# Chunked delta-rule attention with an MLP behind it: one inverse for the first chunk pair, keys apart from queries in three steps, chosen buffer slots, and an order of issue taken from a table

## The chip, the cores and the metric

The kernel runs on one core of one Trainium2 chip. The core has TensorE (PE, with its weight loads PEld), VectorE (DVE), ScalarE (ACT), GpSimd (POOL) and SyncE (SP), which here only issues transfers. Each engine works through its own queue in order and waits on semaphores for the others. The metric is device time in microseconds (us) of one execution of the whole program.

## The reference

`attn` is a recurrent state update for 4 x 8 heads over 768 positions with 48 features; `moe` is a two-layer MLP with softplus on the gated readout.

```python
def _attn_ref(q, k, v, beta, g):              # q k v g: (4, 8, 768, 48), beta: (4, 8, 768)
    k_n = k / (np.linalg.norm(k, axis=-1, keepdims=True) + 1e-06)
    for t in range(S):
        readout = np.einsum('bhd,bhde->bhe', q[:, :, t], state)
        y[:, :, t] = g[:, :, t] * readout
        v_old = np.einsum('bhde,bhd->bhe', state, kt)
        state = state + bt[:, :, :, None] * np.einsum('bhd,bhe->bhde', kt, vt - v_old)

def _moe_ref(x, w_in, w_out):                 # x: (3072, 384), w_in: (384, 2048), w_out: (2048, 384)
    h = x @ w_in
    g = np.maximum(h, 0.0) + np.log1p(np.exp(-np.abs(h)))
    return g @ w_out
```

## The kernel before

The 768 positions are cut into 6 steps (`cc` in the code, counted from 0) of two chunks of 64 positions (`cl`). A chunk is solved at once for all 32 heads. For each step the kernel

- squares and sums the keys (ACT `ksq` L401, DVE `ss` L408), takes 1/norm (ACT Sqrt at L425 in steps 0 and 1, later POOL's pow at L445; DVE L454, L455) and scales the keys to f16 `kn` (L467: DVE, in step 1 POOL); POOL casts the queries to `qn` (L488);
- transposes `kn` and `qn` together on PE (L510) into one PSUM buffer `d`, which ACT copies to `kqt` (L533);
- multiplies keys by keys and keys by queries (the grams, L552 and L556). ACT negates the key part into `kk` (L575); the query part goes through a triangular mask into `mt` (DVE L594; in steps 0 and 1 an ACT copy at L617 and POOL's multiply at L628);
- inverts the small triangular matrices: DVE transposes `kk` into `ln` (L651), two multiplies with beta give `nn` (L675), and 15 pairs of multiply and add (`tmp` L686, `tt` L693) substitute row by row. One such run treats the 16 matrices of a chunk or the 32 of both at the same instruction count. In step 0 the two chunks have runs of their own, the first on DVE and the second on POOL; step 1's run is on DVE and the later ones on POOL;
- brings the result to PE (DVE transposes `tn` L719 and `t` L741, ACT copies), completes the inverse there (X at L775, T at L810 and L820, Z at L862 and L865, with ACT copies `xs`, `td`, `z`);
- runs the chain over the chunks: `w` = v minus keys times state (PE L910, DVE L954; in the first chunk only a copy, L928), `u` in two rounds (PE L968 and L1004, ACT copies L992 and L1035), then new state and readout (PE L1048 and L1058, DVE `s` L1105 and `yg` L1123), and the readout transposed (PE L1141, DVE `xt` L1152);
- runs the MLP: `h` (PE L1176), softplus (ACT `ga` L1197), `o` (PE L1214), a copy (DVE `osb` L1236) and the store. In steps 0 and 5 each chunk is a job of its own, in steps 1 to 4 both chunks are one, so a step's first `h` needs both chunks' `xt`.

q, k, v and g come by SP's queue in the order of the `load` calls, two DMAs of 192 KB for each chunk; the weights come by POOL's queue (L341), each behind a load that is named as its dependency. PE, DVE and the rest get the order of their queues from `Plan`: every piece of work is an item with an engine, an estimated cost, dependencies, buffers and a priority, and `Plan.run` places item after item in the order in which a model of the engines would start them, taking the lowest priority among those that are ready. Priorities are written as 100 times the step plus an offset, with exceptions for steps 0 and 1. Buffers are rings: an item takes the next slot in turn.

## Time and profile before

| | us |
|---|---|
| median of 3 runs | 315.22 |
| lowest, highest run | 311.65, 316.7 |
| the profiled execution's own time | 315.01 |
| its span, first to last instruction | 313.2 |
| mean granted TensorE clock in it | 0.88 of full speed |

The profile is of one execution. Engine busy times overlap, so they don't add up to the span. In timelines a row gives the start in us, the busy time, the engine, the line, the operation with output <- input, shapes (partitions x elements) and how many instructions are merged, and in brackets how long the engine had been idle and what ended that. Matmuls are pipelined, so a merged row's busy time is longer than the distance to the next row. The lines that carry the argument are in the prediction.

### The profile page before, as it was taken

Reading aid. Unit: us, or ns where it says so; the run is one execution under the profiler, and the core shown is the slowest. Engines: PE = TensorE matmul, PEld = TensorE weight load, DVE = VectorE, ACT = ScalarE, POOL = GpSimd, SP = SyncE. Lnnn points to the kernel's source line nnn. Section 1 sums busy time; section 2 is a strip of 40 time slices with the busy share of each in tenths; the row PEclk is TensorE's granted clock in tenths of the full one; section 3 lists DMA queues with packets and bytes.
Section 4 is the critical chain, followed back from the end, with each engine's and each line's share of the span. In section 5 each row is a group of like instructions: output and inputs, shape, how many; then the busy total and the mean of one; then the engine's idle time right before and its main releaser. Section 6 shows DMA issues by size and latency. Waiting matters only on the chain.

```text
span 313.2 us, 13945 instructions
## 1 busy us (share of the span) xinstructions
PE 239.3 (76%) x6384; PEld 159.9 (51%) x6384; DVE 146.1 (47%) x276; ACT 162.0 (52%) x292; POOL 126.4 (40%) x232
## 2 busy tenths in 40 slices
PE   0177302486699989979864989998899989999993
PEld 0056202465568655546554655665455545566761
DVE  2529999892440669253461818363025440133001
ACT  2199703248437655883274476727557156631630
POOL 8919596701072046867860620870005810000000
PEclk9999655569589999998975599999699999999999
DMA  8999999999293188801285490651000220021112
GB/s 118 164 170 159 167 171 178 186 171 160 48 165 70 31 151 165 142 12 46 50 130 86 80 128 12 95 110 47 4 2 4 52 52 4 2 55 34 25 45 53
DMA packets 106860, 27.75 MB, mean 89 GB/s; under 512 B 100784, under 2 KB 106032, under 8 KB 106800
## 3 DMA queue, kind: packets, MB, share of 16 engines
q1 hardware_dynamic: 103680, 23.60, 47.3%
q0 software_dynamic: 3120, 3.24, 6.4%
q8 instruction: 50, 0.82, 1.2%
q14 instruction: 10, 0.08, 0.1%
HBM read 25.26 MB, written 4.72 MB: 96 GB/s over the span
## 4 chain that ended last, share of the span: by engine, by line
PE 56%; DVE 14%; POOL 14%; issue 11%; ACT 4%; DVEq 0%; POOLq 0%; ACTq 0%
PE h L1176 19%; PE o L1214 17%; POOL tt L693 4%; POOL tmp L686 4%; PE d L510 3%; DVE ln L651 2%; DVE tmp L686 2%; PE d L910 2%; PE d L1004 2%; PE d L1058 2%; POOL ss L445 2%; DVE tt L693 2%; PE d L820 2%; PE d L968 2%; DVE nn L675 2%
## 5 line engine op out<-in xcount | busy, mean ns | idle before, releaser
L1197 ACT ACTIVATE ga<-h 128x512 f16<-128x512 f32 x96 | 56.8, 601 | 42.6 <-PE h L1176 39.8
L1176 PE MATMUL h<-xt,w_in 128*128 128x512 f16 (+1 forms) x384 | 75.9, 342 | 2.5 <-DVE xt L1152 1.3
L1214 PE MATMUL o<-w_out,ga 128*128 128x384 f16 x384 | 74.2, 336 | 2.5 <-DVE osb L1236 2.4
L1214 PEld LDWEIGHTS <-ga 128*128 128x128 f16 x384 | 36.9, 100 | 27.7 <-issue 6.5
L1176 PEld LDWEIGHTS <-w_in 128*128 128x128 f16 x384 | 36.5, 101 | 25.8 <-issue 5.9
L445 POOL TENSOR_TENSOR ss<-ss,half_c 128x32 f32<-128x32 f32 x4 | 21.8, 5442 | 35.3 <-DVE ss L408 35.3
L1105 DVE TENSOR_TENSOR s<-d,s 128x384 f16<-128x384 f32 x20 | 10.2, 550 | 50.9 <-PE d L1048 50.9
L1236 DVE COPY osb<-o 128x384 f32<-128x384 f32 x24 | 13.2, 551 | 40.1 <-PE o L1214 40.0
L693 POOL TENSOR_TENSOR tt<-tt,tmp 128x30 f32<-128x30 f32 (+7 forms) x75 | 28.2, 376 | 5.9
L686 POOL TENSOR_TENSOR tmp<-nn,tt 128x30 f32<-128x30 f32 (+7 forms) x75 | 28.0, 373 | 5.6
L533 ACT COPY kqt<-d 128x1024 f16<-128x1024 f16 x24 | 23.8, 1015 | 11.0 <-PE d L510 11.0
L408 DVE TENSOR_REDUCE ss<-ksq 128x16 f32<-128x768 f32 x12 | 11.4, 948 | 29.8 <-ACT ksq L401 29.8
L775 PE MATMUL d<-tn,kk 16*32 16x16 f16 x768 | 8.2, 172 | 20.9 <-ACT tn L729 14.8
L575 ACT ACTIVATE kk<-d 128x256 f16<-128x256 f32 x48 | 16.3, 383 | 15.1 <-PE d L556 13.4
L675 POOL TENSOR_TENSOR nn<-ln,beta_l 128x256 f32<-128x256 f16 x10 | 6.1, 632 | 43.3 <-DVE ln L651 43.3
L510 PE MATMUL d<-ident,kn 128*128 128x128 f16 x96 | 12.1, 264 | 12.8 <-DVE kn L467 10.9
L775 PEld LDWEIGHTS <-kk 16*32 16x32 f16 x768 | 7.4, 92 | 22.4 <-issue 22.2
L510 PE MATMUL d<-ident,qn 128*128 128x128 f16 x96 | 12.2, 262 | 8.0 <-POOL qn L488 4.8
L594 DVE TENSOR_TENSOR mt<-d,mask 128x256 f16<-128x256 f32 x32 | 12.0, 412 | 9.7 <-PE d L556 7.5
L992 ACT CAST u<-d 128x384 f16<-128x384 f32 x24 | 10.4, 485 | 11.8 <-PE d L968 11.8
L552 PE MATMUL d<-kqt 48*64 48x128 f16 x384 | 12.4, 243 | 4.9 <-ACT kqt L533 2.5
L510 PEld LDWEIGHTS <-kn 128*128 128x128 f16 x96 | 8.5, 119 | 13.7 <-DVE kn L467 11.0
(73 smaller groups left out, 371.2 us busy)
## 6 DMA issues: line engine op xcount, KB each, us to landing
kf<-in_k_dram SPq DMA_DIRECT2D x24, 192.0 KB, 5.3
qf<-in_q_dram SPq DMA_DIRECT2D x24, 192.0 KB, 5.3
vf<-in_v_dram SPq DMA_DIRECT2D x24, 192.0 KB, 5.1
gf<-in_g_dram SPq DMA_DIRECT2D x24, 192.0 KB, 5.4
out_dram<-osb SPq DMA_DIRECT2D x48, 96.0 KB, 2.2
w_in<-in_moe_w_in_dram POOLq DMA_DIRECT2D x2, 768.0 KB, 7.6
w_out<-in_moe_w_out_dram POOLq DMA_DIRECT2D x1, 1536.0 KB, 18.7
beta_l<-in_beta_dram POOLq DMA_DIRECT2D x8, 12.0 KB, 4.5
```

What stands on the lines that cost most here:

```text
L445: lambda ss=ss, r=r: nc.gpsimd.tensor_tensor(ss.ap[:, r], ss.ap[:, r], half_c[:, r], ALU.pow),
L510: nc.tensor.transpose(o[:, i, :, j], x.ap[:, p, 2 * i : 2 * i + 2].rearrange("p h d -> p (h d)"), ident,)
L533: lambda tp=tp, kq=kq: nc.scalar.copy(kq.ap.rearrange("p n c -> p (n c)"), f16ps(tp.ap)),
L552: nc.tensor.matmul(o[HALF[r], i], x[:, C:], x)
L575: nc.scalar.activation(kk.ap[:, :, u0 : u0 + 7 : 2].rearrange("p x i t -> p i x t"), g.ap.rearrange("p (i x t) -> p i x t", i=NP, x=4)[:, ...
L686: eng.tensor_tensor(t, nn.ap[:, :, j + 1 :, j : j + 1].broadcast_to([P, 2, n, w]), tt.ap[:, :, j : j + 1, 16 : 16 + w].broadcast_to([P, 2, ...
L693: eng.tensor_tensor(rows, rows, t, ALU.add)
L775: nc.tensor.matmul(uv(xp.ap)[QUAD[qd], u], kk.ap[r, 1, u, :], tn.ap[r, u, :])
L1176: nc.tensor.matmul(hp.ap[:, n * b : n * b + n], w_in[:, j, f * P : (f + 1) * P], xt.ap[:, j, t0 : t0 + n], start=(j == 0), stop=(j == 2),)
L1197: lambda hp=hp, o=gb: nc.scalar.activation(o.ap, hp.ap, AF.Softplus),
L1214: nc.tensor.matmul(op.ap[:, :DM], b.ap[:, c + c0 : c + c0 + 128], w_out[:, f, :], start=(f == 0), stop=(f == NF - 1),)
L1236: lambda op=op, ob=ob: nc.vector.tensor_copy(ob.ap, op.ap[:, :DM]),
```

## The change

Line numbers of the changed kernel are those of its own text (its inverse is at L823, L847, L858 and L865, X at L955, `h` at L1360, `o` at L1398).

1. Step 0 has one inverse for both chunks, on DVE; what follows it (copies, X, T, Z) is still split by chunk (`ends`).
2. In steps 0 to 2 keys and queries are transposed apart, each with copies of half the size, and the grams are two items: keys by keys as soon as the keys are there, queries when they come. The key gram writes its upper half in a matmul of its own, so a step has 192 gram matmuls where it had 128. In step 0 half of the copies of keys go to DVE; the masks of steps 0 and 1 go from POOL to DVE. Step 2's `kn` are scaled on POOL.
3. `kk` is no longer cleared by POOL at the start.
4. The keys of step 1 are loaded ahead of the queries of step 0; the first v and g come chunk by chunk; both halves of w_in wait for the first v and g, w_out for the first v of step 1.
5. One of the two copies of `u` in each round goes from ACT to DVE; the first chunk's `w` goes from DVE to ACT.
6. Rings give out the slot that came free first, by number. Priorities come from `RANK`, a table with a row for each kind of work and a column for each step. `Plan.run` may hold ACT or DVE for an item that is due soon (`WAIT`), counts DVE and POOL as slower beside each other, starts three engines as busy (`BUSY`), and has other limits for PE's groups (`RUN`, `BIG`). None of this is an instruction.

```diff
+    def take(self):
+        self.live += 1
+        x = min(self.freed)
...
+RANK = {
+    "norm": [-722, -1709, -1102, -921, -2682, -1201],
...
+    WAIT = 0.373888
+    BUSY = {"POOL": 8.5, "ACT": 2.3, "DVE": 2.5}
+    RUN = 2
+    BIG = 44
...
+                if e in ("ACT", "DVE"):
+
+                    for r, x in cands:
+                        if x.prio < it.prio - 8 and t0 < r < t0 + self.WAIT * it.cost:
+                            t0, it = r, x
...
-    r_mt = ring("mt", 18, [P, NP, C], F16)
-    r_kk = fixed("kk", 2, [P, 2, U, HC], F16, lambda t: nc.gpsimd.memset(t, 0.0))
+    r_mt = ring("mt", 9, [P, H, C], F16)
+    r_kk = ring("kk", 2, [P, 2, U, HC], F16)
...
     load("k", k, r_k, 0)
+    load("k", k, r_k, 1)
     load("q", q, r_q, 0)
-    load("k", k, r_k, 1)
+    load("v", v, r_v, 0, [0])
+    load("g", g, r_g, 0, [0])
+    weights(w_in[:, :, :FH], w1_hbm[:, :, :FH], ("v", 0, 0), 4.5)
+    weights(w_in[:, :, FH:], w1_hbm[:, :, FH:], ("g", 0, 0), 4.5)
+    load("v", v, r_v, 0, [1])
+    load("g", g, r_g, 0, [1])
     load("q", q, r_q, 1)
...
+    load("k", k, r_k, 2)
+    load("v", v, r_v, 1, [0])
+    load("g", g, r_g, 1, [0])
+    weights(w_out, w2_hbm, ("v", 1, 0), 11.0)
...
-        sc_en, sc_eng = ("POOL", nc.gpsimd) if cc == 1 else ("DVE", nc.vector)
+        sc_en, sc_eng = ("POOL", nc.gpsimd) if cc in (1, 2) else ("DVE", nc.vector)
...
+        other = "DVE" if cc == 0 else "ACT"
+        for cl in cls if cc < 3 else ():
+            kqs = [Buf(r_kqt), Buf(r_kqt)]
+            kqt[cl, 0], kqt[cl, 1] = kqs
+            for j, x, x_it in ((1, kn, kn_it), (0, qn, qn_it)):
+                pj = rk("keys", 6) if j else rk("quer")
+                tp = Buf(p_d)
...
+                def gram_k(kqs=kqs, gp=gp, us=us):
+
+
+                    for p, i, r, m in us:
+                        x = kqs[p].ap[FEAT[m], 2 * i + r, C:]
+                        o = gp[m].ap.rearrange("p (n c) -> p n c", c=2 * HC)
+                        nc.tensor.matmul(
+                            o[HALF[r], NP * p + i],
+                            x,
+                            x[:, None, :HC].broadcast_to([D, 2, HC]),
+                        )
+                    for p, i, r, m in us:
+                        x = kqs[p].ap[FEAT[m], 2 * i + r, C + HC :]
+                        o = gp[m].ap.rearrange("p (n c) -> p n c", c=2 * HC)
+                        nc.tensor.matmul(o[QUAD[2 * r + 1], NP * p + i, HC:], x, x)
+
+                def gram_q(kqs=kqs, gp=gp, us=us):
+                    for p, i, r, m in us:
+                        x = kqs[p].ap[FEAT[m], 2 * i + r]
+                        o = gp[m].ap.rearrange("p (n c) -> p n c", c=C)
+                        nc.tensor.matmul(o[HALF[r], NP * p + i], x[:, C:], x[:, :C])
...
-        groups = [[0], [1]] if cc == 0 else [[0, 1]]
+        groups = [[0, 1]]
+        ends = [[0], [1]] if cc == 0 else groups
...
-            on_dve = cc == 1 or (cc == 0 and gr == [0])
+            on_dve = cc < 2
...
             a4 = [
-                add(
-                    "ACT",
+                evac(
+                    "DVE" if m else "ACT",
                     0.5,
```

What the table does to the queues, at three places. DVE at the first inverse (`ln` the transposed L, `nn` the scaled one, `tt` and `tmp` the substitution, `w` the first chunk's right side). Before:

```order
L651 STREAM_TRANSPOSE ln<-kk_104 128x1024
L454 TENSOR_SCALAR ss<-ss 128x16
L455 RECIPROCAL ss<-ss 128x16
L675 TENSOR_TENSOR nn<-ln,beta_l 128x256 x2
L686 TENSOR_TENSOR tmp<-nn,tt_108 128x30
L693 TENSOR_TENSOR tt_108<-tt_108,tmp 128x2x15
L686 TENSOR_TENSOR tmp<-nn,tt_108 128x56
L693 TENSOR_TENSOR tt_108<-tt_108,tmp 128x2x14x2
L651 STREAM_TRANSPOSE ln<-kk_104 128x1024
L928 CAST w_454<-vf 128x384
L928 CAST w_460<-vf 128x384
L686 TENSOR_TENSOR tmp<-nn,tt_108 128x78
```

and now:

```order
L492 TENSOR_SCALAR ss_160<-ss_160 128x32
L493 RECIPROCAL ss_160<-ss_160 128x32
L549 COPY kqt_241<-d_239 128x8x64
L654 TENSOR_SCALAR kk_168<-d_166 128x8x2x32
L823 STREAM_TRANSPOSE ln_387<-kk_168 128x1024
L847 TENSOR_TENSOR nn_416<-ln_387,beta_l 128x256 x2
L858 TENSOR_TENSOR tmp_425<-nn_416,tt_104 128x30
L865 TENSOR_TENSOR tt_104<-tt_104,tmp_425 128x2x15
L858 TENSOR_TENSOR tmp_425<-nn_416,tt_104 128x56
L865 TENSOR_TENSOR tt_104<-tt_104,tmp_425 128x2x14x2
L858 TENSOR_TENSOR tmp_425<-nn_416,tt_104 128x78
L865 TENSOR_TENSOR tt_104<-tt_104,tmp_425 128x2x13x3
```

The second `ln` and the two `w` have left the run, and it reads one `kk` in which both chunks' keys are written by the rows ahead of it.

POOL in the opening, from its first cast of queries on (`kn` scaled keys, `mt` the masks, `ss` the norms, in the rows of L445 and L483 the pow). Before:

```order
L488 CAST qn_100<-qf 128x16x48
L488 CAST qn_101<-qf 128x16x48
L467 TENSOR_TENSOR kn_94<-kf,ss 128x16x48
L488 CAST qn_100<-qf 128x16x48
L628 TENSOR_TENSOR mt<-mt,mask 128x256 x2
L341 DMA w_in<-in_moe_w_in_dram 128x3x1024
L467 TENSOR_TENSOR kn_95<-kf,ss 128x16x48
L488 CAST qn_101<-qf 128x16x48
L628 TENSOR_TENSOR mt<-mt,mask 128x256 x3
L675 TENSOR_TENSOR nn<-ln,beta_l 128x256 x2
```

and now:

```order
L527 CAST qn_100<-qf_120 128x16x48
L505 TENSOR_TENSOR kn_94<-kf_114,ss_160 128x16x48
L527 CAST qn_101<-qf_123 128x16x48
L505 TENSOR_TENSOR kn_95<-kf_117,ss_160 128x16x48
L387 DMA w_in<-in_moe_w_in_dram 128x3x1024 x2
L837 MEMSET tt_104 128x32x16
L838 COPY tt_104<-beta_l 128x2x16
L527 CAST qn_100<-qf_335 128x16x48
L527 CAST qn_101<-qf_120 128x16x48
L387 DMA w_out<-in_moe_w_out_dram 128x16x384
L483 TENSOR_TENSOR ss_1109<-ss_1109,half_c 128x32
```

The masks are gone, both halves of w_in stand together, w_out stands behind the next clearing of `tt_104`, which the first inverse still uses, and the pow of step 2 behind w_out.

POOL at a later pow. Before, where the inverse of step 3 ends:

```order
L686 TENSOR_TENSOR tmp<-nn,tt_108 128x30
L693 TENSOR_TENSOR tt_108<-tt_108,tmp 128x2x15
L445 TENSOR_TENSOR ss<-ss,half_c 128x32
L665 MEMSET tt_108 128x32x16
L666 COPY tt_108<-beta_l 128x2x16
L445 TENSOR_TENSOR ss<-ss,half_c 128x32
L488 CAST qn_100<-qf 128x16x48
```

and now, near the end of the inverse of step 2:

```order
L865 TENSOR_TENSOR tt_105<-tt_105,tmp_425 128x2x3x13
L483 TENSOR_TENSOR ss_128<-ss_128,half_c 128x32
L858 TENSOR_TENSOR tmp_425<-nn_416,tt_105 128x56
L865 TENSOR_TENSOR tt_105<-tt_105,tmp_425 128x2x2x14
L858 TENSOR_TENSOR tmp_425<-nn_416,tt_105 128x30
L865 TENSOR_TENSOR tt_105<-tt_105,tmp_425 128x2x15
L527 CAST qn_101<-qf_335 128x16x48
L527 CAST qn_100<-qf_120 128x16x48
```

The pow of a later step's norms, which stood behind the whole inverse of step 3, with another right behind it, now stands inside step 2's.

More of the change, by code (lines that the diff above doesn't have):

```diff
@@ L23, in __init__ @@
         self.live = 0
-        self.freed = [0.0] * n
-        self.count = 0
+        self.freed = [(0.0, i) for i in range(n)]
+        self.made = {}
+    def take(self):
+        self.live += 1
+        x = min(self.freed)
+        self.freed.remove(x)
+        if x[1] not in self.made:
+            self.made[x[1]] = self.make(x[1])
+        return x[1], self.made[x[1]]
 class Buf:
@@ L71, in run @@
         issued, arrive = 0, [0.0, 0.0]
+        now = {}
+        for e, t in self.BUSY.items():
+            free[e] = t
         mode, run = "full", 9
@@ L128, in run @@
                 if b.ap is None:
-                    r = b.ring
-                    r.live += 1
-                    r.freed.remove(min(r.freed))
-                    b.ap = r.make(r.count)
-                    r.count += 1
-            it.fn()
+                    b.slot, b.ap = b.ring.take()
+            it.fn()
+            cost = it.cost
+            if e == "POOL" or it.sb:
+                x = now.get("DVE" if e == "POOL" else "POOL")
+                if x is not None and x.sb:
+                    cost += 0.5 * max(0.0, min(x.end - t0, cost))
+            now[e] = it
             if it.dma:
@@ L310, with load @@
     tiles = {}
-    def load(name, x, r, cc):
-        for cl in range(2):
+    def load(name, x, r, cc, cls=(0, 1)):
+        for cl in cls:
             b = Buf(r)
@@ L789 @@
             )
-        for gr in groups:
+        for gr in ends:
             us = slice(16 * gr[0], 16 * gr[-1] + 16)
@@ L1096 @@
             )
+            if first:
+                e3[1].order.append(c1)
             if not final:
```

400 lines of the change are left out of this document (253 added, 147 removed).

## The prediction

> **What bounds the kernel now.** I read the page's head and slices first, then busy time by stretch, then the timeline of the two places where TensorE is idle.
>
> ```profile
> span 313.2 us, 13945 instructions
> PE 239.3 (76%) x6384; PEld 159.9 (51%) x6384; DVE 146.1 (47%) x276; ACT 162.0 (52%) x292; POOL 126.4 (40%) x232
> ...
> PEclk9999655569589999998975599999699999999999
> DMA  8999999999293188801285490651000220021112
> ```
>
> TensorE is busy 76% of the span, but the granted clock is 0.5 to 0.6 in slices 5 to 9 and 0.5 in slices 22 and 23. The busy time by stretch (columns: length, then busy us of PE, PEld, DVE, ACT, POOL, then granted clock, DMA share, GB/s):
>
> ```profile
> 0.00:65.30 65.30, 22.28 (x684) 18.02 (x685) 47.13 (x92) 28.43 (x61) 45.48 (x84) 0.76 1.21 165
> 65.30:90.50 25.20, 19.17 (x721) 14.67 (x721) 10.62 (x23) 14.04 (x23) 7.04 (x6) 0.75 0.76 128
> 90.50:153.90 63.40, 59.50 (x1529) 38.53 (x1527) 31.28 (x57) 40.24 (x72) 34.69 (x68) 0.97 0.47 88
> 153.90:178.40 24.50, 15.88 (x729) 13.34 (x730) 14.46 (x26) 11.77 (x17) 12.68 (x9) 0.62 0.53 88
> 178.40:309.60 131.20, 122.43 (x2734) 75.31 (x2732) 42.66 (x81) 67.48 (x120) 26.52 (x67) 0.97 0.23 44
> ```
>
> From 90.5 to 153.9 and from 178.4 on TensorE is busy 94% and 93% at a clock of 0.97: there it is the bound, and only work taken from it would help. The losses are the opening (43 of 65.3 us idle), the stretch behind it (6.0 of 25.2) and the hole at 153.9 (8.6 of 24.5, the rest at 0.62).
>
> ```profile
> 6.73 3.57 POOL L272 MEMSET kk<- 128x2048 f16 x2
> 14.38 1.60 POOL L488 CAST qn<-qf 128x768 f16<-128x768 f32 x2
> 15.26 0.61 PE L510 MATMUL d<-ident,qn 128*128 128x128 f16 x4 [4.75 <-POOL qn L488]
> 23.63 1.90 DVE L651 STREAM_TRANSPOSE ln<-kk 128x1024 f16<-128x1024 f16 x1
> 26.51 5.08 DVE L675 TENSOR_TENSOR nn<-ln,beta_l 128x256 f32<-128x256 f16 x2
> 46.73 1.04 DVE L719 STREAM_TRANSPOSE tn<-tt 128x512 f32<-128x512 f32 x1
> 48.49 0.66 PE L775 MATMUL d<-tn,kk 16*32 16x16 f16 x64 [11.98 <-ACT tn L729]
> 54.77 0.21 PE L865 MATMUL d<-td,kk 32*32 32x32 f16 x3 [2.53 <-issue]
> 61.51 0.31 PE L1048 MATMUL d<-u,kn 64*64 64x48 f16 x8 [3.44 <-issue]
> 65.33 3.33 PE L1176 MATMUL h<-xt,w_in 128*128 128x256 f16 x18 [0.65 <-DVE xt L1152]
> ```
>
> The opening is a chain. POOL clears kk and reaches the queries at 14.38, and the joint transposes of keys and queries wait for them (4.75). VectorE transposes the first L at 23.63 and needs until 46.73 for one chunk's inverse; its two scalings (nn) alone take 5.08 while POOL works on the same kind of tensors, and POOL runs the second chunk's inverse beside it. TensorE then waits 11.98 for tn. From tn to the first h are 18.6 us, 2.53 and 3.44 of them waits that no other engine ends ("issue").
>
> ```profile
> 155.65 5.44 POOL L445 TENSOR_TENSOR ss<-ss,half_c 128x32 f32<-128x32 f32 x1
> 163.03 0.61 PE L510 MATMUL d<-ident,kn 128*128 128x128 f16 x4 [0.97 <-DVE kn L467]
> 178.36 1.49 PE L1176 MATMUL h<-xt,w_in 128*128 128x512 f16 x3
> ```
>
> In the hole the o of step 1 has run out and the first h of step 2 comes 24.5 us later: its second chunk's chain stands in TensorE's queue behind the next keys, which wait for POOL's pow at 155.65.
>
> **The change, part by part.** Prices of VectorE alone, of a gram and of the loads:
>
> ```profile
> 50.79 1.14 DVE L675 TENSOR_TENSOR nn<-ln,beta_l 128x256 f32<-128x256 f16 x2
> 58.14 0.33 DVE L686 TENSOR_TENSOR tmp<-nn,tt 128x128 f32<-128x128 f32 x1
> 67.34 0.22 DVE L686 TENSOR_TENSOR tmp<-nn,tt 128x110 f32<-128x110 f32 x1
> 69.77 0.19 DVE L693 TENSOR_TENSOR tt<-tt,tmp 128x30 f32<-128x30 f32 x1
> 6.90 0.95 DVE L408 TENSOR_REDUCE ss<-ksq 128x16 f32<-128x768 f32 x1 [4.42 <-ACT ksq L401]
> 8.89 0.96 DVE L467 TENSOR_TENSOR kn<-kf,ss 128x768 f16<-128x768 f32 x1
> 9.17 0.84 ACT L401 ACTIVATE ksq<-kf 128x768 f32<-128x768 f32 x1 [1.06 <-DMA kf<-in_k_dram]
> 9.83 4.66 SPq L319 DMA_DIRECT2D kf<-in_k_dram  x4
> 30.85 0.30 PE L556 MATMUL d<-kqt 48*32 48x64 f16 x16
> 43.55 10.30 SPq L319 DMA_DIRECT2D kf<-in_k_dram  x4
> ```
>
> *Start of the inverse.* The keys of both pairs are loaded first. The second half of k lands at about 9.15 (ScalarE's wait at 9.17) and four DMAs take 4.66, so each later chunk follows 2.33 behind: 11.5 and 13.8 for the next keys, 16.1 and 18.5 for the first queries. The clearing of kk (3.57) and the queries leave the path. What gates now is ScalarE's and VectorE's order: the Square of the next keys (0.84) stands ahead of the first kqt copy, so that copy and the second chunk's root wait for 12.4. From reduce to the end of kn VectorE took 2.95 (6.90 to 9.85), so the second kn is at 15.3. Behind it come two of the four-transposes of 0.61, a copy behind the next pair's reduce and reciprocal, the gram (64 matmuls, 1.2 at 0.30 for 16, twice that at half clock) and the copy to kk: I take 5.4 for them, so 20.7 for the one transpose of L, which now waits for both chunks (bounds 19.5, and 23.6, the old start). At 1.90 it ends at 22.6.
>
> *One inverse.* nn costs 1.14. Ten late steps took 2.62 from 67.34 to 69.96, 0.26 each; the widest took 0.36 from start to start behind 58.14. Thirty at about 0.29 are 8.8: it ends at 32.6, against 46.73, and POOL stands still meanwhile, since its next clear of tt waits for it. Bounds: if POOL still took turns, the old 20.2 from 26.51, so 42.8; and 30.5 if all thirty went at the pitch of 0.22.
>
> *From tn to the first h.* Before 18.6. Ahead of the first h the order now has 944 matmuls, 684 before: the second chunk's X and T, the queries' grams and the next pair's. They lie largely where TensorE waits for copies; I take 1 us for them. VectorE also takes half the copies of u, and the masks that were POOL's; ScalarE takes the copies of w. That gives 32.6 + 19.6 = 52.2, or 13.1 earlier. Bounds: without the two issue waits 46; with one more of 3.4 and a late load 58. The load: VectorE's reduce for step 2's keys stands between yg and the new state, and those keys are the fifth load behind the first g (18.5 + 4.7 = 23.2). At 2.33 each they land at 35, at the slowest pace shown (10.30 for four DMAs, beside the weights) at 49, where about 45 is needed.
>
> *The weights.*
>
> ```profile
> w_in<-in_moe_w_in_dram POOLq DMA_DIRECT2D x2, 768.0 KB, 7.6
> w_out<-in_moe_w_out_dram POOLq DMA_DIRECT2D x1, 1536.0 KB, 18.7
> 45.54 1.18 POOL L341 DMA_DIRECT2D w_out<-in_moe_w_out_dram  x1
> 69.83 0.81 PE L1214 MATMUL o<-w_out,ga 128*128 128x384 f16 x4
> ```
>
> w_out was there at 45.54 + 18.7 = 64.2, ahead of its first use at 69.83. It now waits for step 1's first v, the seventh load behind 23.2: 39.5, and with w_in's two 768 KB at the pace of the loads (8 x 1.17) 48.8. So it lands near 67.5. Ahead of the first o stand 398 matmuls behind the first h; at the rate of the third stretch (1529 in 63.4) 16.5, so 68.7. It costs nothing, and that cover is thin: each us beyond it is a us.
>
> *Behind the first h.* The stretch to 90.5 lost 6.0 idle and ran at 0.75. Now it holds no o and one chunk's chain; I take 3 less (bounds 6 less, 3 more).
>
> *The hole.*
>
> ```profile
> 117.74 0.44 PE L910 MATMUL d<-s,kqt 48*64 48x48 f16 x32
> 121.11 1.20 POOL L675 TENSOR_TENSOR nn<-ln,beta_l 128x256 f32<-128x256 f16 x2 [2.05 <-DVE ln L651]
> 137.71 1.25 DVE t L741 x2
> ```
>
> Steps 2 to 4 get keys, pow and gram earlier, and the longest run of matmuls without h or o in the order falls from 728 (24.5 us) to 502, now between steps 0 and 1. By count that is 16.9, so 7.6 less; the 226 moved go between h and o at 0.44 for 32, 3.1 in all. So 4.5 saved (bounds 0, if the new hole is as long, and 14.6, if it closes to its work at full clock: 15.88 at 0.62 is 9.8, of which 502/728 are 6.8; 24.5 - 6.8 - 3.1).
>
> *Added grams.* 192 more matmuls at 0.30 for 16. The first two steps' lie in the opening; the third's 64 cost 1.2, I take 1 (bounds 0 and 3.6). Buffer slots and the planner's new rules issue nothing. The third step's two kn go from VectorE to POOL, idle there.
>
> Sum against the profiled execution: 313.2 - 13.1 - 3.0 - 4.5 + 1.0 = 293.6. Its own time was 315.01, 1.8 more, and stands 0.2 under the median of 315.22. So 295.4, told as 295.
>
> On the issue waits the Trainium skill speaks against me ("Runtime: NRT & Kernel Launch", Instruction fetch mechanics): TensorE's instructions come in blocks and the crossing is "mostly hidden". By it the path from tn would be 6.0 shorter and the time 289; the rows 2.53 and 3.44 show it not hidden while DMA is full, so I keep them.
>
> **The rivals.**
> (a) Nothing waits again: first h at 46 (19.3 gained), 6 behind it, 14.6 in the hole: 313.2 - 19.3 - 6 - 14.6 + 1 + 1.8 = 276, and up to 288 if only part of it comes. For it: in the last stretch no other engine is over 52%. Against: every stretch with small matmuls shows issue waits.
> (b) The hole is only moved: 24.5 us at another place, so 300 (295.4 + 4.5). For it: TensorE runs its queue in order, and the 128 X matmuls of step 2 stand inside the new run.
> (c) The loads bound the opening, since the DMA slices read 9 or more up to slice 10: keys of step 2 at 49, first h at 58: 295.4 + 5.8 = 301, and 304 if w_out is 3 later still. The Trainium skill ("DMA: Bandwidth & Descriptors", Issuing engines are not separate DMA queues) has all queues on the same engines, so that early weights delay the rest; 10.30 against 4.66 agrees.
> (d) Slower: POOL's inverse of step 2 began at 121.11 and its last transposes at 137.71. In the new order the X matmuls of step 2 stand ahead of any h of step 1. 1234 matmuls after the first h the new hole begins, by the same rate at 52.2 + 51 = 103, and X, half-way in it, is due at 111. POOL's inverse now has the next pow (5.44) in its midst, so X is ready 16.6 + 5.4 + 2.4 (transposes, copy) = 24.4 after it starts: a start after 87 delays all that follows, one after 113 makes the kernel slower, and the old 121.11 would give 295 + 34 = 329. Against: its grams stand right behind the first o, with 12 o, the gram, kk and 1.90 of transpose before it, so I expect the start near 77.
> (e) No change: the chain from kn to the first h keeps 60 us or more, 309 to 321; only if VectorE's inverse still takes turns with POOL (10.2 later) and (b) holds.
>
> **How the numbers follow.** Forecast 0.43; (a) 0.18, (b) 0.18, (c) 0.12, (d) 0.03, (e) 0.06. A measurement can tell about 2%, here 308.9 and 321.5. All but (d) and (e) are faster: 0.91; same 0.06; slower 0.03. The range reaches from 281, which leaves out the lower half of (a), to 305: with (d) and (e) 0.18 are outside.
>
> **What would show it.** Right: VectorE's first nn near 1.1, tn near 33, first h between 46 and 58, w_out landed before the first o, POOL's inverse of step 2 before 90, a hole under 20 us between o of step 0 and h of step 1, clock 0.95 or more behind it. Wrong: the inverse over 15 us, X of step 2 waiting for tn, or idle TensorE behind h in a wait for keys.

## The result, and the profile after

| | before | after | predicted |
|---|---|---|---|
| median of 4 runs each, us | 314.62 | 294.69 | 295.0 |
| lowest to highest | 311.65 to 316.7 | 292.62 to 294.87 | 281 to 305 |
| ratio after/before, 95% interval | | 0.938 (0.930 to 0.947) | |
| profiled execution, its span | 315.01, 313.2 | 294.87, 293.2 | |
| first `h` in the profile | 65.33 | 55.15 | 52.2 |
| the hole without `h` or `o` | 24.5 | 17.2 | 16.9 |

A few executions of a kernel run over 1.5% longer than its fastest; the ratio above, and each time and ratio that is given for a run below, is from the mean of the others (before 313.63, the changed kernel 294.22).

The time came out as forecast, but two terms of the sum were off by about 3 us each, in opposite directions, and the experiments show that a part of the gain has another cause than the prediction gave.

The page of the changed kernel, head and slices:

```profile
span 293.2 us, 14316 instructions
PE 236.2 (81%) x6576; PEld 159.3 (54%) x6576; DVE 146.6 (50%) x298; ACT 151.6 (52%) x257; POOL 102.5 (35%) x182
...
PEclk9997555557995995779999999999999999999999
DMA  8999999978989159920297901551100121021212
```

Its busy time by stretch (columns as in the prediction: length, then busy us of PE, PEld, DVE, ACT, POOL, then granted clock, DMA share, GB/s). The stretches are the opening, the one up to the first `o`, the one up to the last `o` of step 0, the hole, and the rest:

```profile
0.00:55.15 55.15, 22.79 (x945) 19.19 (x945) 36.66 (x90) 28.43 (x52) 24.09 (x35) 0.73 1.19 161
55.15:74.40 19.25, 16.72 (x406) 12.68 (x400) 8.89 (x27) 9.65 (x18) 4.01 (x3) 0.61 0.94 155
74.40:106.40 32.00, 28.36 (x838) 18.71 (x835) 16.60 (x29) 15.21 (x25) 19.69 (x38) 0.89 0.65 117
106.40:123.50 17.10, 10.53 (x499) 9.16 (x502) 10.02 (x17) 10.78 (x13) 2.40 (x5) 0.73 0.94 163
123.50:290.00 166.50, 157.79 (x3916) 99.53 (x3908) 74.42 (x137) 87.50 (x150) 52.27 (x104) 0.99 0.29 55
```

From 123.5 on TensorE is busy 157.79 of 166.5 us (95%) at a clock of 0.99; before it was 93% at 0.97. In the 123.5 us ahead of that it is busy 78.4, and the clock is 0.61 to 0.73 in three of the four stretches. The record of the clock begins with its first change, here at 22.26, so the 9s ahead of that are no measurement: eight transposes take 1.04 at 10.81, as long as at 41.80, and 0.61 at 72.11 (rows of the timeline below). So the 0.73 of the first stretch is too high. The timeline of the changed kernel, from VectorE, TensorE and POOL at the places that the prediction named:

```profile
10.81 1.04 PE L566 MATMUL d<-ident,kn 128*128 128x128 f16 x8 [10.81 <-DVE kn L505]
...
20.13 1.92 DVE L823 STREAM_TRANSPOSE ln<-kk 128x1024 f16<-128x1024 f16 x1
22.09 0.76 DVE L847 TENSOR_TENSOR nn<-ln,beta_l 128x256 f32<-128x256 f16 x2
26.99 0.29 DVE L858 TENSOR_TENSOR tmp<-nn,tt 128x128 f32<-128x128 f32 x1
31.63 1.03 DVE L893 STREAM_TRANSPOSE tn<-tt 128x512 f32<-128x512 f32 x1
...
33.38 0.66 PE L955 MATMUL d<-tn,kk 16*32 16x16 f16 x64 [3.72 <-ACT tn L905]
41.80 1.03 PE L566 MATMUL d<-ident,qn 128*128 128x128 f16 x8 [3.63 <-POOL qn L527]
54.13 0.51 PE L1000 MATMUL d<-td,xs 32*16 32x16 f16 x49 [4.07 <-issue]
55.15 2.74 PE L1360 MATMUL h<-xt,w_in 128*128 128x256 f16 x12
60.88 0.39 PE L1148 MATMUL d<-w,td 32*32 32x48 f16 x21 [2.52 <-issue]
65.91 2.74 PE L1360 MATMUL h<-xt,w_in 128*128 128x256 f16 x12
72.11 0.61 PE L566 MATMUL d<-ident,kn 128*128 128x128 f16 x8
74.36 1.95 PE L1398 MATMUL o<-w_out,ga 128*128 128x384 f16 x11
...
43.67 1.18 POOL L387 DMA_DIRECT2D w_out<-in_moe_w_out_dram  x1
80.67 1.20 POOL L847 TENSOR_TENSOR nn<-ln,beta_l 128x256 f32<-128x256 f16 x2 [1.33 <-DVE ln L823]
...
113.57 0.61 PE L955 MATMUL d<-tn,kk 16*32 16x16 f16 x59 [0.34 <-issue]
118.12 0.53 PE L1000 MATMUL d<-td,xs 32*16 32x16 f16 x53 [0.52 <-issue]
123.22 0.52 PE L1090 MATMUL d<-s,kqt 48*64 48x48 f16 x25 [3.68 <-issue]
```

L starts at 20.13 (before 23.63), both nn take 0.76 (5.08), tn is there at 31.63 (46.73). From there to the first `h` are 23.5 us, where 18.6 stood before. The waits that no other engine ends are still there: 4.07 and 2.52 around the first `h`, 3.68 in the hole.

### The profile page after: what moved, and what is told of

It is laid out like the page before. It is cut to its first block, busy times and chain, and to the rows that moved or that the text cites. A ratio compares the mean times of both kernels' runs of the same rounds, so it can differ in the third digit from the quotient of the medians.

```text
span 293.2 us, 14316 instructions
## 1 busy us (share of the span) xinstructions
PE 236.2 (81%) x6576; PEld 159.3 (54%) x6576; DVE 146.6 (50%) x298; ACT 151.6 (52%) x257; POOL 102.5 (35%) x182
## 4 chain that ended last, share of the span: by engine, by line
PE 72%; SPq 11%; issue 8%; DVE 4%; DMA 2%; POOL 1%; ACT 0%; DVEq 0%; POOLq 0%
PE h L1360 24%; PE o L1398 22%; SPq L365 11%; PE d L1090 3%; PE d L1148 2%; PE d L711 2%; PE d L955 2%; PE d L1240 2%; PE d L1000 2%; DMA qf<-in_q_dram 2%; PE d L1045 2%; PE d L1185 2%; PE d L752 2%; PE d L1325 2%; PE d L1230 1%
## 5 line engine op out<-in xcount | busy, mean ns | idle before, releaser
L1360 PE MATMUL h<-xt,w_in 128*128 128x512 f16 (+1 forms) x384 | 77.5, 346 | 0.0
L1398 PE MATMUL o<-w_out,ga 128*128 128x384 f16 x384 | 73.3, 331 | 1.8 <-DVE osb L1420 1.5
L1398 PEld LDWEIGHTS <-ga 128*128 128x128 f16 x384 | 35.7, 99 | 24.3 <-issue 2.9
L1360 PEld LDWEIGHTS <-w_in 128*128 128x128 f16 x384 | 36.9, 103 | 21.7 <-issue 1.1
L549 DVE CAST u<-d 128x384 f16<-128x384 f32 x24 | 13.4, 556 | 37.5 <-PE d L1185 18.9
L483 POOL TENSOR_TENSOR ss<-ss,half_c 128x32 f32<-128x32 f32 x4 | 21.9, 5475 | 28.5 <-DVE ss L446 28.5
L865 POOL TENSOR_TENSOR tt<-tt,tmp 128x30 f32<-128x30 f32 (+7 forms) x60 | 23.5, 392 | 4.7
L858 POOL TENSOR_TENSOR tmp<-nn,tt 128x30 f32<-128x30 f32 (+7 forms) x60 | 21.3, 355 | 4.6
L1134 DVE TENSOR_TENSOR w<-vf,d 128x384 f16<-128x384 f32 x22 | 11.1, 547 | 11.2 <-PE d L1090 10.2
L547 ACT COPY kqt<-d 128x512 f16<-128x512 f16 x22 | 11.9, 590 | 8.3 <-PE d L566 8.3
L439 ACT ACTIVATE ksq<-kf 128x768 f32<-128x768 f32 x12 | 10.2, 846 | 11.6 <-DMA kf<-in_k_dram 9.1
L847 POOL TENSOR_TENSOR nn<-ln,beta_l 128x256 f32<-128x256 f16 x8 | 4.8, 622 | 31.7 <-DVE ln L823 31.7
L1000 PE MATMUL d<-td,xs 32*16 32x16 f16 x768 | 8.6, 167 | 8.9 <-issue 8.8
L1307 DVE TENSOR_TENSOR yg<-d,gf 128x384 f16<-128x384 f32 x24 | 12.2, 547 | 6.2 <-ACT ga L1381 3.5
L734 ACT COPY kqt<-d 128x1024 f16<-128x1024 f16 x12 | 12.1, 1014 | 5.8 <-PE d L711 5.8
L566 PE MATMUL d<-ident,kn 128*128 128x128 f16 x48 | 5.3, 278 | 11.7 <-DVE kn L505 11.7
L527 POOL CAST qn<-qf 128x768 f16<-128x768 f32 x12 | 9.8, 828 | 13.3 <-DMA qf<-in_q_dram 11.2
L955 PE MATMUL d<-tn,kk 16*32 16x16 f16 x768 | 8.1, 171 | 7.0 <-ACT tn L905 3.7
## 6 DMA issues: line engine op xcount, KB each, us to landing
w_out<-in_moe_w_out_dram POOLq DMA_DIRECT2D x1, 1536.0 KB, 15.3
```

Of the source, the lines that this page charges most:

```text
L483: lambda ss=ss, r=r: nc.gpsimd.tensor_tensor(ss.ap[:, r], ss.ap[:, r], half_c[:, r], ALU.pow),
L547: nc.scalar.copy(d, x)
L549: nc.vector.tensor_copy(d, x)
L858: eng.tensor_tensor(t, nn.ap[:, :, j + 1 :, j : j + 1].broadcast_to([P, 2, n, w]), tt.ap[:, :, j : j + 1, 16 : 16 + w].broadcast_to([P, 2, ...
L865: eng.tensor_tensor(rows, rows, t, ALU.add)
L955: nc.tensor.matmul(uv(xp.ap)[QUAD[qd], u], kk.ap[r, 1, u, :], tn.ap[r, u, :])
```

## The experiments

Before's mean beside these runs was 312.67 to 314.11, and 313.63 beside the changed kernel. So times are compared with 294.22 as they stand, and a difference of 1 us is not told apart. The intervals are those of the ratio to before; the changed kernel's is 0.930 to 0.947.

### Which part of the change pays

Two kernels replace the table of order by the rule of the kernel before; the planner then orders everything anew. The second also puts keys and queries back into one transpose.

```diff
-    "norm": [-722, -1709, -1102, -921, -2682, -1201],
-    "pow": [-726, 401, -1276, -1902, -1287, -380],
+    "norm": [-70, -104, 130, 230, 330, 430],
+    "pow": [-120, -154, 80, 180, 280, 380],
...
```

```diff
-        for cl in cls if cc < 3 else ():
+        for cl in cls if cc < 3 and not 0 <= cc < 3 else ():
...
-        for cl in cls if cc > 2 else ():
+        for cl in cls if cc > 2 or 0 <= cc < 3 else ():
```

> The change without its table of order: the ranks are computed by the rule of the kernel before, all other edits stay. Theory T (the gain of the opening comes from the one inverse on VectorE and keys apart from queries, whatever sets the order): first h at 55 to 60, at most 302 us. Rival U (the table makes the gain): first h beyond 60 or a hole of over 24 us again, 308 us or more.

> As the run with the old rule of order, and keys and queries of the first three steps are transposed together again (the split undone). To be held against that run. T: the first transposes wait for the first queries (about 17 in place of 11), the transpose of L starts 2 to 6 later and the time is 2 to 6 us longer. Rival: the second chunk's keys and ScalarE's order gate L anyway, under 1 us.

Measured: 308.10 us, ratio 0.981 (0.970 to 0.992), and 304.50 us, 0.969 (0.959 to 0.980). The first h came at 62.3 and 66.0. So all other edits together are worth about 5 us under the old rule, and the table another 14: rival U holds. The split of keys and queries moves the first h by 3.7 and the time by nothing that can be told apart; the 2 to 6 us longer of T did not come. The table can't be tried without the other edits, which it was made for, so this is no sum of two independent gains.

The granted clock of the run with the old rule bears on half of its 14 us:

```profile
PEclk9997555569999959999959779899999985999999
```

Its first h is 7.2 later than the changed kernel's, and what lies behind it 6.7 longer. There TensorE stands idle as long in both (20.6 us up to 303.0, against 20.1 up to 288.6), but the matmuls take 220.1 us in place of 213.4, and the clock lapses until 262, where the changed kernel's is at half for the last time at 128. The mean clock there is 0.91 against 0.92, too near to account for all of the 6.7.

Two more took back one edit each under the table: two inverses in step 0, and the old order of loads.

```diff
-    r_kk = ring("kk", 2, [P, 2, U, HC], F16)
+    r_kk = fixed("kk", 2, [P, 2, U, HC], F16, lambda t: nc.gpsimd.memset(t, 0.0))
...
-        groups = [[0, 1]]
+        groups = [[0], [1]] if cc == 0 else [[0, 1]]
...
-            on_dve = cc < 2
+            on_dve = cc == 1 or (cc == 0 and gr == [0])
...
```

```diff
     load("k", k, r_k, 0)
+    load("q", q, r_q, 0)
     load("k", k, r_k, 1)
-    load("q", q, r_q, 0)
...
+    weights(w_out, w2_hbm, ("g", 0, 1), 11.0)
...
-    weights(w_out, w2_hbm, ("v", 1, 0), 11.0)
...
```

> The changed kernel with the first step's inverse taken apart again: the first chunk's on VectorE, the second's on POOL, and kk cleared by POOL at the start (L is transposed chunk by chunk). T (the whole pair's inverse on VectorE pays because POOL's half came late and held up VectorE): nn back above 1.5 each, the second chunk's tn behind 50, 3 to 8 us longer than the changed kernel. Rival: the second chunk's chain binds nothing before the first o, within 2 us.

> The changed kernel with the loads in the order of the kernel before (each step whole, w_out behind step 0's g). T: queries of step 0 and keys of step 1 change places, so the first steps of norms come apart, but L hangs on the second chunk's keys of step 0: between 1 us shorter and 4 us longer. Rival (the order of the loads is what lets the inverse start at 20): ln at 23 or later and 3 us or more longer.

Measured: 314.26 us (ratio 1.003, 0.997 to 1.009) and 312.69 us (0.998, 0.994 to 1.003); no theory had this. The edit can't be told from what came with it: with other items the same table gives another order everywhere. The slices of the kernel with two inverses, in its profiled execution (318.29):

```profile
PE   0352479456499985999888799999796999999893
PEclk9996556757579996699959879999659899999999
```

Its first h came at 48.2, 7 us ahead of the changed kernel's, and it is still 20 slower: behind its first 48 h stands a stretch of 30.4 us (56.7 to 87.1) with 692 matmuls and neither h nor o, a second one of 12.4 us follows at 114.7, and the clock reads 5 to 7 in 15 of the 40 slices, where the changed kernel has 11. In the other kernel L even starts earlier, at 19.2, so there the old order of loads did not hold the inverse up; its holes are 22.6 and 12.4 us. An early first h is no gain by itself. Both runs say nothing on the price of their edit, and the later ones therefore keep the changed kernel's order: it is recorded item by item and replayed, with the named edit alone.

### The inverse: what it costs, and why it is short

In one kernel ten reductions of 768 elements stand behind the last step of step 0's inverse on VectorE, in the other 28 multiplies of 128x128 on POOL behind the issue of w_in's second half.

```diff
+    e = [x for x in seq if x.eng == "DVE" and x.cost == 1.4][0]
+    i = seq.index(e.deps[0])
...
+    for n in range(10):
+        x = Item()
+        x.eng, x.bufs = "DVE", []
+        x.fn = lambda: nc.vector.tensor_reduce(pb, pa.broadcast_to([P, 16, 48]), mybir.AxisListType.X, ALU.add)
+        seq.insert(i + 1, x)
```

```diff
+    i = seq.index(wl[1])
...
+    for n in range(28):
+        x = Item()
+        x.eng, x.bufs = "POOL", []
+        x.fn = lambda: nc.gpsimd.tensor_tensor(pb, pb, pa, ALU.mult)
+        seq.insert(i + 1, x)
```

> The changed kernel in its own order on every engine, with ten reductions of 0.95 (nothing uses what they write) behind step 0's inverse on VectorE, so that tn comes about 9.5 later, near the 42.8 at which the prediction's bound for an inverse that takes turns with POOL had it. T (tn sets the start of the rest): 3.6 of it disappear in the wait for step 1's queries at 41.80, so first h 6 later and the time 6 longer (near 301), or up to 9.5. Rival (the issue waits or the loads set the start): first h less than 3 later, time within 2 of the changed kernel.

> The changed kernel in its own order, with 28 multiplications of a 128x128 half-precision tile on POOL (nothing uses them) behind the issue of w_in, beside VectorE's inverse. T (VectorE's nn of 5.08 for two was long because POOL worked on SBUF at the same time): nn back over 1.5 for the two, the inverse over 11 in place of 9.5, time 1 to 5 longer. Rival (nn was long only because of POOL's own inverse and its buffers): nn stays at 0.76, the time the same.

A longer inverse: tn came at 41.65, 10.0 later, the first h at 65.1, 9.9 later, and the time was 301.65 (ratio 0.960, 0.951 to 0.970), 7.4 more. So tn does set the start, and about three quarters of this delay arrive at the end. The wait for the queries at 41.80 was gone, as expected, but the 3.6 did not disappear with it: another wait of TensorE's own (2.88) took its place.

A busy POOL: tn came at 37.84, 6.2 later, the first h at 61.2, 6.1 later, but the first o at 75.9, only 1.6 later, and the time was 295.36 (0.940, 0.930 to 0.951), which can't be told from the changed kernel's. So a delay in the opening does not reach the end by a fixed share. The timelines of VectorE and POOL in that run:

```profile
22.57 0.76 DVE L846 TENSOR_TENSOR nn<-ln,beta_l 128x256 f32<-128x256 f16 x2
23.74 0.48 DVE L864 TENSOR_TENSOR tt<-tt,tmp 128x30 f32<-128x30 f32 x1
30.39 0.47 DVE L857 TENSOR_TENSOR tmp<-nn,tt 128x128 f32<-128x128 f32 x1
36.88 0.47 DVE L864 TENSOR_TENSOR tt<-tt,tmp 128x56 f32<-128x56 f32 x1
37.39 0.19 DVE L857 TENSOR_TENSOR tmp<-nn,tt 128x30 f32<-128x30 f32 x1
37.84 1.03 DVE L892 STREAM_TRANSPOSE tn<-tt 128x512 f32<-128x512 f32 x1
...
23.20 14.08 POOL L1442 TENSOR_TENSOR pb<-pb,pa 128x128 f16<-128x128 f16 x28
```

While POOL's 28 multiplies run (0.427 each, one per 0.50), nearly all of VectorE's take 0.45 to 0.49, whether they have 30 elements or 128, and one comes per 0.51; alone they took 0.19 to 0.29. When POOL is done the next takes 0.19. The two engines take turns, one instruction each. The inverse took 15.3 in place of 9.5. So the mechanism behind the prediction's bound for an inverse that still takes turns is shown, at a smaller price than the bound of 20.2, whose run before also held the second transpose of L and two copies of w: the gain is not the one instruction stream for two chunks alone, but that POOL stands still beside it. Both nn took 0.76 here too, since POOL's multiplies began at 23.20, behind them; so what made nn take 5.08 before was not tried. The Trainium skill ("Trainium Architecture — The Big Picture", What this means for kernel authors) calls the pair's port an exclusive lock, not a split of bandwidth; the equal 0.47 for every size agrees.

### The waits that nobody ends

In each run these waits stand a multiple of 128 matmuls apart. Between the rows 113.57, 118.12 and 123.22 above stand 128 matmuls each; so do 54.13 and 60.88. With a weight load each that is 256 instructions, and the page counts 51 transfers of instructions with 0.84 MB in all, 16 KB each, where 6576 matmuls are 51.4 such blocks. The packed traces date these transfers, and they settle what ends the waits: in all fourteen kernels each of the 224 waits of over 0.3 us at the start of a block ends 1.2 to 1.9 us after a transfer has landed, the first block's after the first transfer, and so on in step. The waits of 4.07 and 2.52 end at 54.13 and 60.88; their transfers landed at 52.59 and 59.47. The planner of both kernels already prices this (3.5 us for each 128 matmuls); the prediction named the fetch and kept the waits, but did not count in blocks. Two kernels move transfers in the recorded order, the queries of step 1 in the first and w_out in the second; a third stands by itself.

```diff
+    four = [tiles[x][1] for x in (("v", 0, 1), ("g", 0, 1), ("q", 1, 0), ("q", 1, 1))]
+    at = [seq.index(x) for x in four]
+    for p, n in zip(at, (2, 3, 0, 1)):
+        seq[p] = four[n]
```

```diff
+    i, j = seq.index(wl[2]), [n for n, x in enumerate(seq) if x.eng == "POOL" and x.cost == 5.6][0]
+    seq.insert(j, seq.pop(i))
```

> The changed kernel in its own order on all engines but SP, where the two loads of step 1's queries stand ahead of v and g of step 0's second chunk. T (those queries, late at POOL, hold TensorE 3.63 at 41.80): that wait goes below 1 and the first h comes 2 to 3.6 earlier, 1 to 3.5 gained in all. Rival (the wait only moves, since v and g come later by as much, or the fetch of TensorE's instructions takes it back): first h within 1 of 55.15 and the time within 1.

> The changed kernel in its own order on all engines but POOL, where the load of w_out stands behind step 2's pow (about 56 in place of 43.7). T (the issue waits of 4.07 and 2.52 are fetches of TensorE's instructions that queue behind w_out's 1.5 MB): they shrink by half, first h 1 to 3 earlier, w_out lands near 71, ahead of the first o at 74.36, 1 to 3 gained. Rival (the loads of q, k, v and g fill the DMA engines anyhow): the waits stay, time within 1, or longer by what w_out comes late.

The first of them failed as an experiment: 299.49 us (0.953, 0.945 to 0.962). The second chunk's queries of step 1 use the buffer of step 0's first chunk, and in this order they are written there before POOL has read it (so this kernel's first chunk works on wrong queries); POOL's first cast waited for that load, 16.46 us until 28.14, and L started at 31.88. Whether the queries of step 1 can profitably come earlier stays open.

The second: 293.30 us, ratio 0.934 (0.926 to 0.942), 0.9 less than the changed kernel, which its interval does not tell apart; the 1 to 3 gained that T expected are not shown. TensorE's timeline there:

```profile
50.02 0.51 PE L999 MATMUL d<-td,xs 32*16 32x16 f16 x49 [0.44 <-issue]
51.03 2.74 PE L1359 MATMUL h<-xt,w_in 128*128 128x256 f16 x12
54.57 0.39 PE L1147 MATMUL d<-w,td 32*32 32x48 f16 x21 [0.32 <-issue]
58.85 0.30 PE L1184 MATMUL d<-u,z 32*32 32x48 f16 x11 [1.24 <-issue]
70.30 2.08 PE L1397 MATMUL o<-w_out,ga 128*128 128x384 f16 x6 [3.16 <-DMA w_out<-in_moe_w_out_dram]
```

The same two matmuls that waited 4.07 and 2.52 now wait 0.44 and 0.32. The 128 between them take 4.55 (50.02 to 54.57) in place of 6.75 (54.13 to 60.88), and the first h comes 4.1 earlier. The rival falls: w_out's 1.5 MB delayed the instructions, although the loads of q, k, v and g fill the DMA engines in both. The transfer itself took 1.05 beside w_out and 1.18 without it; what w_out held up was its start, 4.85 after the block ahead of it began in place of 1.47. A new wait came, of o for w_out until 70.30 (3.16), but that first o is still 4.1 ahead of the changed kernel's, and the first h of step 1 3.8 ahead, at 119.89. Of these 3.8 the profiled execution lost 1.7 behind that h, at a clock of 0.97 where the changed kernel has 0.98.

The kernel by itself issues this twice, 1536 matmuls each, first with no wait on the 24 loads and then behind the last of them:

```python
for i in range(n):
    r = QUAD[i % 4]
    c = 16 * ((i // 4) % 32)
    nc.tensor.matmul(o[r, c : c + 16], x[r.start : r.start + 16, :32], x[r.start : r.start + 16, 32:48])
```

> A kernel by itself that computes nothing of the reference: 1536 matmuls of 16x32 weights by 16 columns while 24 tiles are loaded from q, k, v and g, and 1536 more, with a wait for the last load before them, while nothing is transferred. T (TensorE's instructions come 128 matmuls at a time by DMA and queue behind the loads): in the first part a wait of 2 to 4 before every 128th matmul, in the second part under 1. Rival (the wait hangs on how fast the matmuls are used up, not on the loads): the same wait in both parts.

Its timeline on TensorE, three rows with loads and three without:

```profile
25.36 1.32 PE L48 MATMUL d<-a 16*32 16x16 f16 x128 [3.35 <-issue]
29.91 1.32 PE L48 MATMUL d<-a 16*32 16x16 f16 x128 [3.23 <-issue]
34.74 1.19 PE L48 MATMUL d<-a 16*32 16x16 f16 x128 [3.51 <-issue]
...
71.28 1.19 PE L48 MATMUL d<-b 16*32 16x16 f16 x128 [2.27 <-issue]
75.28 1.19 PE L48 MATMUL d<-b 16*32 16x16 f16 x128 [2.81 <-issue]
79.29 1.19 PE L48 MATMUL d<-b 16*32 16x16 f16 x128 [2.81 <-issue]
```

128 small matmuls take 1.2 to 1.3 us, and the next 128 start 4.55 later on average with loads (51.57 less 6.06, over 10) and 3.73 without (105.11 less 67.83, over 10). So the expectation was wrong and the rival mostly right: the wait is there without any load (2.15 to 2.81), and the loads add 0.8. That the waits look long only where DMA is full comes from what runs there: idle DMA goes with large h and o matmuls, of which 128 last longer than a fetch (13.95 us from 262.58 on). What fits all runs: in a long stretch of small matmuls TensorE gets 128 per 3.7 us with no transfers, per 4.0 to 5.1 beside the loads, and per 6.7 to 7.4 beside w_out (46.69 to 54.13 and 54.13 to 60.88). These are averages of a long stretch: one block is fetched ahead, so the first 223 of the kernel by itself ran without a wait, and in the changed kernel a block of 7.21 (136.01 to 143.22) was followed by one of 2.97.

### The hole and the clock

Three more in the recorded order. In the first w_out comes late, in two halves, and the last 16 o matmuls of step 0 are spread into the hole; in the second five reductions stand ahead of a copy on VectorE; in the third 6, 8 and 8 matmuls stand ahead of three groups of the opening.

```diff
+            nc.gpsimd.dma_start(out=w_out[:, r], in_=w2_hbm[:, r])
...
+    oi = [x for x in pe if x.mm == 4][12:16]
...
+    for x, at in zip(oi, (h[1], h[3], h[6], h[12])):
+        seq.insert(seq.index(at) + 1, x)
```

```diff
+    i = seq.index([x for x in seq if x.eng == "DVE" and x.cost == 0.56][14])
...
+    for n in range(5):
...
+        seq.insert(i, x)
```

```diff
+    for x, n in ((pe[i - 2], 6), (pe[i], 8), (pe[j], 8)):
...
+            for _ in range(n):
+                nc.tensor.matmul(
+                    b.ap.rearrange("p (a c) -> p a c", a=4),
+                    ident,
+                    ident[:, None].broadcast_to([P, 4, P]),
+                )
+            f()
```

> The changed kernel's order with three moves: the load of w_out behind step 2's pow, in two halves (the run with the late load waited 3.16 for the whole of it), and the last 16 o matmuls of step 0 spread into the hole. T: o waits under 1.2 for w_out, the hole's waits of 0.94, 1.08 and 3.68 shrink by 2 to 3 in all under the o between them: 288 to 291. Rival (the hole is paced by VectorE's and ScalarE's copies of step 1, which then come 3.4 after the o as before): 292 to 294, as the run with the late load alone.

> The changed kernel in its own order, with five reductions of 0.95 (nothing uses them) on VectorE ahead of one copy of o near 237, so that TensorE waits about 4 once, in the stretch that ran at a clock of 0.99. T (an idle TensorE loses its clock and pays again when it starts): granted clock near 0.5 for some us behind it, time 6 to 9 longer. Rival: the wait alone, 4 longer, or less if later waits shrink.

> The changed kernel in its own order, with 22 matmuls of 128x128 by 512 that nothing uses, ahead of three groups of the opening that wait 2.65, 3.72 and 3.63 (at about 26, 33 and 42); each writes a PSUM tile that the group then overwrites. T (the opening and the first h run at half clock because TensorE idles): h x12 at 1.48 in place of 2.74 from the start, 3 to 7 gained. Rival (the small matmuls take as long at either clock and waits set the pace): first h within 1 of 55.15, the time within 2; or up to 3 longer where the added ones outlast the waits.

The filled hole: 294.33 us, ratio 0.942 (0.935 to 0.948). No gain over the run with the late load, as its rival said, but not for its reason: the first h of step 1 came at 122.80, and the waits in the hole were again at every 128th matmul (1.33, 0.38, 2.71). The hole is paced by the fetch: two of its waits, 1.33 at 112.69 and 2.71 at 122.34, end 1.4 to 1.7 after a transfer of instructions has landed, and the o matmuls that were put into it count among the 128. w_out's second half was still waited for, 1.61.

The reductions went wrong in place: a cost of 0.56 also marks other work of VectorE, and they ran at 95.2, not near 237. TensorE waited 3.44 at 101.11. Up to there this kernel's order is the changed one's, and yet it was ahead, with the first h at full clock by 65 in place of 70:

```profile
54.29 2.74 PE L1359 MATMUL h<-xt,w_in 128*128 128x256 f16 x12
65.06 1.49 PE L1359 MATMUL h<-xt,w_in 128*128 128x256 f16 x12
71.71 2.11 PE L1397 MATMUL o<-w_out,ga 128*128 128x384 f16 x12
```

So two executions of one order differ by 0.9 at the first h and by 2.65 at the first o. Behind the wait the hole began 1.3 later than the changed kernel's (107.77 against 106.50) and ended 0.5 later (124.19 against 123.67), so it gave back 0.8. The time was 299.39 (0.958, 0.949 to 0.966), 5.2 more, which does not decide between the 4 of the rival and the 6 to 9 of T. In the profiled execution 3.2 us were lost behind the hole, in the clock. The same place in the changed kernel and then in this run:

```profile
194.06 0.18 PE L955 MATMUL d<-tn,kk 16*32 16x16 f16 x3 [1.66 <-issue]
194.18 1.47 PE L1398 MATMUL o<-w_out,ga 128*128 128x384 f16 x8
```

```profile
195.68 0.20 PE L954 MATMUL d<-tn,kk 16*32 16x16 f16 x3 [2.21 <-issue]
195.81 2.74 PE L1397 MATMUL o<-w_out,ga 128*128 128x384 f16 x8
```

After a fetch wait of 1.66 eight o matmuls take 1.47; after one of 2.21 they take 2.74. The granted clock was 1.00 there in the one and 0.50 in the other, from 194.8 to 201.6; at half clock these 6.8 us do the work of 3.4, by this estimate as much as was lost. Which waits cost the clock can't be read off their length alone in these runs.

The added matmuls: 291.05, 293.39, 298.21 and 298.87 us, from which no ratio can be told. In the profiled execution (span 289.3) the first h stayed at 55.36, with a fetch wait of 3.18 before it, but the h that ran at half clock until 70 ran at full clock from 60:

```profile
53.79 0.25 PE L1089 MATMUL d<-s,kqt 48*64 48x48 f16 x3 [3.18 <-issue]
55.36 2.69 PE L1359 MATMUL h<-xt,w_in 128*128 128x256 f16 x12
60.37 1.48 PE L1359 MATMUL h<-xt,w_in 128*128 128x256 f16 x12
70.15 2.11 PE L1397 MATMUL o<-w_out,ga 128*128 128x384 f16 x12
```

The first o came 4.2 ahead of the changed kernel's, but only 1.6 ahead of the one at 71.71 above, which had no matmuls added. What the clock is worth there is therefore not shown: two executions of one order differ by more than half of it, and the four times of this kernel by 8. No version tried beats the changed kernel by more than its runs differ.

## Why the prediction came out right

**Start of the inverse** (20.7, measured 20.13) and **one inverse** (ends 32.6, measured 31.63): right in size and in cause. POOL's turns are shown by the run with the busy POOL. That the keys' loads come first was part of the working; the old order of loads gave 19.2 in another plan, so this step is not shown.

**From tn to the first h** (19.6, measured 23.5): off by 3.9, and the term at fault is the weights. "It costs nothing, and that cover is thin" asked only when w_out lands, not what it holds up. Beside it the two blocks around the first h took 7.44 and 6.75; with w_out later 4.10 and 4.55, and from tn to the first h it was 19.2 (31.88 to 51.03), and 19.7 in the run with the filled hole, as forecast. So the 1 us for 260 more matmuls, two more blocks, is not refuted. The wait of 3.63 for step 1's queries lay in the same time; its own share was not found, since that experiment failed. So the opening gave 10.2, not 13.1.

**The weights** (w_out near 67.5): it was issued at 43.67, 5 earlier than reckoned, and landed 15.3 later, near 59, well ahead of the first o. It did no harm as a late load but as an early one. The rule of the Trainium skill that rival (c) named ("DMA: Bandwidth & Descriptors", Issuing engines are not separate DMA queues) agrees: the 6.75 in place of 4.55 fell on TensorE's instructions.

**The hole** (16.9, measured 17.2): right, for a reason that the prediction lacked. It scaled the old 24.5 by the number of matmuls, 502 against 728. That holds because the hole is paced by fetches: 502 matmuls are 3.9 blocks, in 14.9 to 18.0 us in the seven runs that keep this order up to there. The Trainium skill ("Runtime: NRT & Kernel Launch", Instruction fetch mechanics) says "mostly hidden"; for small matmuls about 2.5 of 3.7 us are not hidden even with DMA idle.

**Behind the first h, and added grams** (-3.0 and +1.0, with the hole -6.5): measured 247.9 before and 238.05 after, -9.85. Of this TensorE's idle time is 6.3 (30.9 before, 24.6 now) and its busy time 3.6. For the 3.3 us more than forecast the clock of 0.99 in place of 0.97 over the last 166 us would account (2% of 166, an estimate), which no run shows by itself. The prediction had no term for it, and it is the least certain part: the same order gave 291 to 299 us with 22 more matmuls.

**What the sum hid**: it took each us by which the first h comes earlier as a us of the time. The runs don't bear that out: a first h 9.9 later cost 7.4; 6.1 later cost 1.1 and 4.1 earlier gave 0.9, neither of them told from nothing; and 7 earlier in another order came with 20 more. It also priced the edits and took the order for granted, and the run with the old rule shows that 14 of the 20 us hang on the order. Half of that was seen as an earlier first h, half as less busy time behind it, whose cause stays open; that the order does it by short runs of small matmuls between h and o is a reading that no run tests. In the changed kernel fetch waits of up to 1.66 remain behind 128 us, but no lapse of the clock. That 295.0 met 294.69 is luck, since two misses of 3 us cancel.

The rivals: (a) fell with the fetch; (b) fell, the hole is shorter by a third; (c) and (d) fell, step 2's `ss` was there at 50.63 and POOL's inverse began at 80.67, ahead of 87, though (c) was right that early weights delay what follows; (e) has for its lower end about what this change gave under the old rule of order (308.1).

## What to carry to other kernels

Count matmuls, not only their time: a long stretch of small ones on TensorE can't go faster than its instructions come, here 128 in 3.7 us on average and up to 5.1 beside loads, so look for such stretches between the large ones, and for big transfers beside them: moving one brought the first h 4.1 earlier here, though the time did not follow. Price an operation on VectorE by whether POOL works beside it. And when a planner orders the work, test an edit with the order held fixed, since otherwise two orders are compared and not two edits. Even then one profile of each is little: two executions of one order differed by 2.65 us at the first o.

## What was not expected of the hardware

Instructions for TensorE came per 128 matmuls in 3.73 us on average with no other transfers, 4.55 beside the loads of 192 KB, and up to 7.44 beside one load of 1.5 MB, and each wait for them ended 1.2 to 1.9 us after 16 KB had landed. VectorE and POOL alternated one instruction each, about 0.47 for VectorE's whatever its size. And a wait of 2.21 us was followed by half the clock where one of 1.66 was not. The Trainium skill ("TensorE: Matmul & The Clock Gate", What's actually happening) speaks of a free-running window of about 3.4 us, which would make this a matter of where the wait falls. The traces agree on the window: the changes of the granted clock lie whole multiples of 3.41 us apart in each of the thirteen kernels that have any. What decides within one is not shown: TensorE was busy for 80% of the 3.41 us ahead of one drop to half clock (145.17, in the run with the old rule and joint transposes) and for 51% of a stretch after which the clock stayed up (to 167.10, in the run with added matmuls).
